# Four of 128 stores of a decode-attention backward kernel sent as 126 + 2 partitions, to choose the DMA engines that carry them

## The chip, the cores and the metric

The kernel runs on one core of one Trainium2 chip. The metric is the device time of that core in microseconds (us), as the median of several executions. "Engine" is used for two things: the compute engines (PE is TensorE, DVE is VectorE, ACT is ScalarE, POOL is GpSimd, SP is SyncE) and the 16 DMA engines that move data for the core. Where it matters I write "DMA engine".

## The reference, cut to what matters

```python
B, H, Sq, Sk, D = 2, 32, 1, 8192, 128          # q, grad_out: 1 row a head; k, v: 8192 rows a head; bf16
def forward(q, k, v):
    scores = einsum("bhqd,bhkd->bhqk", q, k) * D ** -0.5
    return einsum("bhqk,bhkd->bhqd", softmax(scores), v)
out, vjp = jax.vjp(forward, q, k, v)
return (out, *vjp(grad_out))                    # out, dq, dk, dv
```

There are 64 heads. For each the kernel loads 2 MB of k and 2 MB of v and stores 2 MB of dk and 2 MB of dv: 268 MB in and 268 MB out.

## The kernel before

Each tile holds one head's k or v: 128 partitions of 64 x 128 bf16, 16 KB a partition. I call such a partition a row. The outer product that gives dk or dv overwrites the same tile, which is then stored. There are 12 tile slots, so the load for head i + 6 waits until the store of head i has landed. SyncE issues the loads and GpSimd issues the stores.

```python
NTILE = 12
load_eng = nc.sync
store_eng = nc.gpsimd
...
def load(i, w, pieces=(NCH,)):
    t = kvp.tile([P, NT, D], BF16, tag=f"kv{slot_of(i, w)}", name="kvt")
    h.tile[w] = t
    src = (v_v if w else k_v)[i]
    ...
        pin(load_eng.dma_start(out=t[:, n0:n1, :], in_=src[:, n0:n1, :]))
...
def outer(i, w, c, ends):
    pin(nc.vector.tensor_tensor(out=h.tile[w][...], in0=h.qb[w][...], in1=h.pair[w][...], op=ALU.mult))
    if c + 1 in ends:
        ...
        dst = (dv_v if w else dk_v)[i]
        pin(store_eng.dma_start(out=dst[:, b0:b1, :], in_=h.tile[w][:, b0:b1, :]))
...
        if (i := at(O1 + NCH)) is not None and i + AHEAD < BH:
            load(i + AHEAD, 0)
        if (i := at(O0 + NCH)) is not None and i + AHEAD < BH:
            load(i + AHEAD, 1)
        if x := within(O1):
            outer(x[0], 1, x[1], last if x[0] == BH - 1 else whole)
        if x := within(O0):
            outer(x[0], 0, x[1], last if x[0] == BH - 1 else whole)
```

## Time and profile before

| | before |
|---|---|
| time, median (range) | 1304.45 us (1304.21 to 1306.08, 4 runs) |
| span of the profiled run | 1303.1 us |
| busiest compute engine (PE) | 89% |
| the two data queues, share of 16 DMA engines | 48.9% + 48.7% |
| mean DMA rate | 414 GB/s |

These are lines of the page of the kernel before: the busy time of each compute engine, the DMA's busy tenths and rate in 40 equal slices of the span, the queues (packets, MB, share), and two groups of DMA issues (last column: median us from issue to landing).

```profile
span 1303.1 us, 42566 instructions
PE 1154.0 (89%) x19268; PEld 873.0 (67%) x19268; DVE 937.5 (72%) x2122; ACT 974.8 (75%) x641; POOL 72.4 (6%) x142
...
DMA  9999999999999999999999999999999999999965
GB/s 390 423 427 427 427 427 427 428 426 430 427 427 427 427 427 429 427 428 427 429 427 427 429 427 424 418 420 425 421 416 420 419 421 421 418 421 422 394 281 206
...
q1 hardware_dynamic: 19040, 268.51, 48.9%
q0 software_dynamic: 19296, 268.44, 48.7%
...
out_dram<-kvt POOLq DMA_DIRECT2D x126, 2048.0 KB, 40.4
kvt<-in_v_dram SPq DMA_DIRECT2D x64, 2048.0 KB, 49.3
```

The DMA is busy from the second slice to the last two. For 24 slices it moves about 427 GB/s (423 to 430 in slices 2 to 24), then about 420, and the last three slices show 394, 281 and 206. So the DMA bounds the kernel. The busy digits 6 and 5 of the last two slices are means over 16 engines: some have run out of work before others, as the landings of the last store below show (3 us on fifteen engines, 10 on one).

Waits on the kernel before: the queue of SyncE (columns: engine and line, what it waited for, us in total, times, longest).

```profile
SPq L89 <- DMA out_dram<-kvt: 1140.6, 116, 24.2
```

```profile
POOL out_dram L390 <- DVE kvt L376: 1186.8, 127, 32.2
```

SyncE spends nearly the whole span waiting for stores to land, since a landed store is what frees a tile for the next load; it never waits longer than 24.2 us.

The trace has one semaphore update for each DMA engine and DMA, 16 in all. Their times after the issue show the engines apart (my reading of the trace, us, in order of landing):

```
before, load  issued at 1003.10: 12 12 12 12 12 13 14 | 28 28 29 29 29 30 31 32 | 49
before, store issued at 1001.50: 12 12 13 13 13 14 16 | 19 20 20 21 21 21 21 21 | 42
before, last store at   1291.64: 3 (fifteen engines)                            | 10
```

Seven engines are early, eight are later, and one is alone at the end. I call it the slow engine. It is the one that is still busy when the kernel ends.

Its packets can be followed in the trace, because on a DMA engine that has work the next packet's record mostly starts 3 or 4 ns before the end of the one before. Which packet follows which is sometimes ambiguous, so what is said below of single engines is a reading, not a view of the profile. The slow engine's packets have no gap from about 140 us to the end. A 16 KB row takes 0.607 us from start to start at full pace.

### The profile page before, as it was taken

To read this page: it belongs to the slowest core of one execution; us is meant where nothing else is said; L and a number is where in the kernel's file an instruction comes from. 1 tells how busy PE (TensorE), PEld (TensorE's weight loads), DVE (VectorE), ACT (ScalarE), POOL (GpSimd) and SP (SyncE) were. 2 spreads that over 40 slices of the span, in tenths; PEclk is the share of its full clock that TensorE was granted. 3 is DMA by queue.
4 is the path that set the end of the run, shared out by engine and by line. 5 is a ranking of instruction groups with operands and counts; after the bars stand their busy time and mean duration, and the time that the engine had idled before them with its cause. 6 is when DMAs were issued, how large, how long until landed. Compare 5 with 4: busy or idle time off the path is not lost.

```text
span 1303.1 us, 42566 instructions
## 1 busy us (share of the span) xinstructions
PE 1154.0 (89%) x19268; PEld 873.0 (67%) x19268; DVE 937.5 (72%) x2122; ACT 974.8 (75%) x641; POOL 72.4 (6%) x142
## 2 busy tenths in 40 slices
PE   6999998889898888988989888989898898888984
PEld 5777776667676666666766666667676676666662
DVE  2888887677776777767777677676776767777776
ACT  6888887777787777777778777777777777777771
POOL 0000000000000000000000000000000000000001
PEclk9999999899898999989989999898898989999986
DMA  9999999999999999999999999999999999999965
GB/s 390 423 427 427 427 427 427 428 426 430 427 427 427 427 427 429 427 428 427 429 427 427 429 427 424 418 420 425 421 416 420 419 421 421 418 421 422 394 281 206
DMA packets 38517, 539.67 MB, mean 414 GB/s; under 512 B 4544, under 2 KB 4544, under 8 KB 5824
## 3 DMA queue, kind: packets, MB, share of 16 engines
q1 hardware_dynamic: 19040, 268.51, 48.9%
q0 software_dynamic: 19296, 268.44, 48.7%
q8 instruction: 150, 2.46, 0.7%
q14 instruction: 31, 0.25, 0.0%
HBM read 268.47 MB, written 268.47 MB: 412 GB/s over the span
## 4 chain that ended last, share of the span: by engine, by line
issue 80%; DMA 11%; POOL 4%; DVE 2%; PE 1%; POOLq 0%; SPq 0%; DVEq 0%
DMA kvt<-in_v_dram 8%; POOL out_dram L390 4%; DMA out_dram<-kvt 3%; DVE kvt L376 1%; PE tp L166 1%; POOLq L390 0%; PE acc L321 0%; DVE sel L344 0%; PE dpw L177 0%; SPq L89 0%; SPq L96 0%; DVE sel L338 0%; PE sw L177 0%; PE acc L358 0%; DVE pair L252 0%
## 5 line engine op out<-in xcount | busy, mean ns | idle before, releaser
L168 ACT COPY ev<-tp 128x2048 bf16<-128x2048 bf16 x512 | 954.0, 1865 | 300.3 <-PE tp L166 290.6
L166 PE MATMUL tp<-ident_bf,kvt 128*128 128x128 bf16 x8192 | 573.4, 226 | 108.9 <-DMA kvt<-in_v_dram 91.1
L376 DVE TENSOR_TENSOR kvt<-qb,pair 128x2048 bf16<-128x2048 bf16 x512 | 621.1, 1214 | 0.2
L166 PEld LDWEIGHTS <-kvt 128*128 128x128 bf16 x8192 | 501.4, 102 | 116.2 <-DMA kvt<-in_v_dram 95.8
L177 PEld LDWEIGHTS <-ev 128*128 128x128 bf16 x8192 | 242.8, 96 | 211.2 <-issue 164.4
L321 PE MATMUL acc<-kvt,dS_pad 128*64 128x512 bf16 x1024 | 177.2, 430 | 1.3 <-DVE dqT L361 1.3
L321 PE MATMUL acc<-kvt,E_pad 128*64 128x512 bf16 x1024 | 159.8, 392 | 0.0
L177 PE MATMUL dpw<-qdT,ev 128*128 128x1 bf16 x4096 | 140.9, 164 | 12.0 <-DVE qb L159 10.7
L189 DVE TENSOR_REDUCE mp<-sw 128x1 f32<-128x64 f32 x64 | 14.3, 224 | 186.5 <-PE sw L177 186.5
L344 DVE SCALAR_TENSOR_TENSOR sel<-acc,diag,sel 128x128 f32<-128x128 f32 x384 | 134.6, 351 | 13.6
L177 PE MATMUL sw<-qdT,ev 128*128 128x1 bf16 x4096 | 142.5, 164 | 1.1 <-ACT ev L168 1.1
L390 POOL DMA_DIRECT2D out_dram<-kvt x134 | 71.3, 532 | 1219.2 <-DVE kvt L376 1186.8
L321 PEld LDWEIGHTS <-dS_pad 128*64 128x64 bf16 x1024 | 38.5, 113 | 26.9 <-issue 9.4
L229 DVE CAST E_pad<-E_f 128x64 bf16<-128x64 f32 x64 | 12.5, 195 | 60.6 <-ACT E_f L220 60.6
L321 PEld LDWEIGHTS <-E_pad 128*64 128x64 bf16 x1024 | 36.3, 108 | 21.0 <-issue 0.2
L358 PE MATMUL acc<-ones,sel 128*128 128x1 f32 x256 | 43.3, 239 | 6.2 <-DVE sel L344 6.2
L264 PE MATMUL dpw<-ld,ones 128*128 128x1 f32 x256 | 46.3, 250 | 0.1
L338 DVE TENSOR_SCALAR sel<-acc,diag 128x128 f32<-128x128 f32 x128 | 44.0, 344 | 0.0
L358 PEld LDWEIGHTS acc<-ones,sel 128*128 128x128 f32 x256 | 39.0, 193 | 7.3 <-DVE sel L344 7.3
L235 DVE CUSTOM_DVE_ANT_0 junk<-E_f,dpw 128x64 bf16<-128x64 f32 x64 | 14.1, 220 | 40.2 <-PE dpw L177 40.2
L159 DVE CAST qb<-dpw 128x128 bf16<-128x128 f32 x128 | 35.4, 277 | 6.0 <-PE dpw L150 6.0
L264 PEld LDWEIGHTS dpw<-ld,ones 128*128 128x128 f32 x256 | 38.2, 188 | 0.5 <-DVE ld L235 0.5
(42 smaller groups left out, 303.2 us busy)
## 6 DMA issues: line engine op xcount, KB each, us to landing
out_dram<-kvt POOLq DMA_DIRECT2D x126, 2048.0 KB, 40.4
kvt<-in_v_dram SPq DMA_DIRECT2D x64, 2048.0 KB, 49.3
kvt<-in_k_dram SPq DMA_DIRECT2D x63, 2048.0 KB, 49.4
out_dram<-kvt POOLq DMA_DIRECT2D x8, 512.0 KB, 11.3
kvt<-in_k_dram SPq DMA_DIRECT2D x2, 512.0 KB, 4.5
kvt<-in_k_dram SPq DMA_DIRECT2D x1, 1024.0 KB, 7.1
out_dram<-nat SPq DMA_DIRECT2D x2, 16.0 KB, 5.0
qd_nat<-in_q_dram SPq DMA_DIRECT2D x1, 16.0 KB, 6.8
```

Source lines behind the costliest of these rows:

```text
L159: pin(nc.vector.tensor_copy(out=h.qb[w][:], in_=h.qbp))
L166: pin(nc.tensor.transpose(tp[:, t, :], src[:, c * CH + t, :], ident_bf[:]))
L168: pin(nc.scalar.copy(out=ev[:], in_=tp[:]))
L177: nc.tensor.matmul(dst[:, c * CH + t : c * CH + t + 1], lhsT=ev[:, t, :], rhs=qdT[:, w, i : i + 1], start=True, stop=True,)
L189: pin(nc.vector.reduce_max(out=h.mp[:], in_=h.s, axis=AX.X))
L264: nc.tensor.matmul(out, lhsT=ones[:].to_broadcast([P, P]), rhs=col, start=True, stop=True)
L321: nc.tensor.matmul(h.acc[w][g : g + CW, :], lhsT=wts[:, n0 : n0 + CW], rhs=rows[:, n0 : n0 + QT, :].rearrange("p n d -> p (n d)"), start=( ...
L338: nc.vector.tensor_scalar(out=h.sel[:], in0=block, scalar1=diag[:, 0:1], scalar2=None, op0=ALU.mult)
L344: nc.vector.scalar_tensor_tensor(out=h.sel[:], in0=block, scalar=diag[:, b : b + 1], in1=h.sel[:], op0=ALU.mult, op1=ALU.add,)
L358: nc.tensor.matmul(h.acc[w][:, 0:1], lhsT=h.sel[:], rhs=ones[:], start=True, stop=True)
L376: nc.vector.tensor_tensor(out=h.tile[w][:, n0 : n0 + CH, :].rearrange("p n (e t) -> p n e t", t=2), in0=h.qb[w][:] .rearrange("p (e t) -> ...
L390: pin(store_eng.dma_start(out=dst[:, b0:b1, :], in_=h.tile[w][:, b0:b1, :]))
```

## The change

```diff
+            if w == 0 and i % 14 == 9 and ends is whole:
+                spread(dst, h.tile[w])
+            else:
+                pin(store_eng.dma_start(out=dst[:, b0:b1, :], in_=h.tile[w][:, b0:b1, :]))
+
+    def spread(dst, t):
+
+        def eighths(ap, m):
+            parts = ap[P - 1 : P].rearrange("p (e m n) d -> p m e (n d)", e=8, m=2)
+            return parts[:, m]
+
+        pin(store_eng.inc_swdge_sem([], [], mode="reset_dge_cursor"))
+        pin(store_eng.dma_start(out=eighths(dst, 0), in_=eighths(t, 0)))
+        pin(
+            store_eng.dma_start(
+                out=dst[: P - 2], in_=t[: P - 2], max_dma_last_dim=NT * D
+            )
+        )
+        pin(load_eng.dma_start(out=eighths(dst, 1), in_=eighths(t, 1)))
+        pin(load_eng.dma_start(out=dst[P - 2 : P - 1], in_=t[P - 2 : P - 1]))
```

## The prediction

Engines 6 and 7 were to be left out. The "it" that "keeps about 29 us" is the slow engine. The sum is 1304.2 - 19.4 + about 1 = 1286 us; its 19.4 us, an estimate from the pitch in the trace (4 stores x 8 rows x 0.607 us), counts only if the slow engine is left out.

> **What bounds the kernel.** The DMA engines. The page's slices show DMA at 9 of 10 up to the last two; the two data queues take 48.9% and 48.7% of 16 engines' span. PE is 89% busy, others less. SyncE's queue waits 1140.6 us for stores to land, as tiles are reused.

> Not all 16 engines bind. The trace has 16 semaphore updates for each DMA, one an engine. For loads and stores issued around 100 us they lie within about 4 to 8 us; around 1000 us seven land 12 to 14 us after a load's issue, eight after 28 to 32, and one alone after 49. The gap grows until about 800 us; then the slow engine holds back tile reuse, and GB/s falls from 427 to 420. Every 8 loads take 77.8 us before (128 packets of 16 KB at a pitch of 0.607 us) and about 81 after. I conclude that one engine is busy from 4 us to the end with about 48 us more than the fastest, and 20 us more than the next eight. It alone sets the time.

> **What the change does.** An ordinary store gives an engine 8 rows, 8 x 0.607 = 4.86 us. [...] So engines 6 and 7 save 4 x 4.86 = 19.4 us and the others gain 4 x 0.607 = 2.4 us, plus little for the two rows. No trace names an engine; [...] Then it keeps about 29 us over the fastest and the next eight about 24: it still binds, and all of the 19.4 us counts.

> **What it costs.** SyncE sends the rest in order: after a load that waits for the store of dv of the same head, and the next load waits for these rows to land. They lie behind the loads queued on the slow engine (49 us): four times the next load comes some 40 us late, and the load queue runs empty for about 2 us. The fast engines idle then, at no cost, as they were ahead; the slow one has four stores queued. I allow 0 to 2 us for each of the four.

> **Prediction.** 1304.2 - 19.4 + about 1 = 1286 us, 1.4% faster; range 1279 to 1304. Chances: faster by over 2% 0.05, within 2% 0.92, slower 0.03.

> **What would show it.** Right: in the stores concerned 14 engines take 9 rows and two take one small piece; after each of the four places the spread of landings falls to a few us, and one load is issued about 40 us late; the mean rate rises to about 420 GB/s. Wrong: the last landing still trails by about 20 us on the same schedule.

> **What would make it wrong.** The slow engine is not 6 or 7, or the store of 126 partitions goes over 16 engines after all: then 1304 to 1310. The late loads starve PE or drain the store queue as well, up to 10 us each. Or the next eight engines bind sooner.

## More of the kernel before

GpSimd waits for DVE's outer products, never for a DMA.

On the slow engine the store packets take a median of 0.644 us while it also reads loads, where the median of the other engines is 0.611.

## The result and the profile after

| | before | after |
|---|---|---|
| time, median (range) | 1304.45 us (1304.21 to 1306.08, 4 runs) | 1308.98 us (1308.24 to 1309.07, 4 runs) |
| ratio after / before, 95% interval | | 1.0031 (1.0013 to 1.0048) |
| span of the profiled run | 1303.1 us | 1306.5 us |
| granted PE clock in it | 0.944 | 0.955 |

An interval that leaves out 1 shows a difference. Ratios here and below are the mean time of one kernel's runs over that of the other's in the same rounds, so they are not quite the ratio of the medians. The kernel is 0.3% slower, where 1.4% faster was predicted.

These are the lines of the page of the kernel after that answer to those of before, with the new groups of DMA issues (126 rows are 2016 KB; half of a row is 8 KB).

```profile
span 1306.5 us, 42590 instructions
...
DMA  9999999999999999999999999899999999999965
GB/s 389 423 426 427 428 427 427 427 427 428 427 426 428 429 425 428 420 414 427 426 429 428 427 425 424 364 427 427 428 428 428 427 423 421 370 429 428 428 275 206
...
q0 software_dynamic: 20064, 268.35, 48.6%
...
out_dram<-kvt POOLq DMA_DIRECT2D x122, 2048.0 KB, 47.8
out_dram<-kvt POOLq DMA_DIRECT2D x4, 2016.0 KB, 51.4
out_dram<-kvt POOLq DMA_DIRECT2D x4, 8.0 KB, 35.9
```

The last two slices are as before (275 and 206 against 281 and 206): the end still trails. The dips to 414, 364 and 370 are new. They follow three of the four places.

The next fence has the queue of SyncE in the kernel after, as waits; the two behind it show this queue's issues around the third place as a timeline (start in us, duration, line, transfer), first before, then after.

```profile
SPq L89 <- DMA out_dram<-kvt: 1140.3, 108, 43.8
```

```profile
809.98 0.33 SPq L89 DMA_DIRECT2D kvt<-in_v_dram  x1
820.22 0.33 SPq L89 DMA_DIRECT2D kvt<-in_k_dram  x1
830.44 0.33 SPq L89 DMA_DIRECT2D kvt<-in_v_dram  x1
840.54 0.33 SPq L89 DMA_DIRECT2D kvt<-in_k_dram  x1
```

```profile
805.50 0.33 SPq L89 DMA_DIRECT2D kvt<-in_k_dram  x1
805.93 1.56 SPq L409 DMA_DIRECT2D out_dram<-kvt  x1
807.54 0.42 SPq L410 DMA_DIRECT2D out_dram<-kvt  x1
843.57 0.34 SPq L89 DMA_DIRECT2D kvt<-in_v_dram  x1
844.02 0.36 SPq L89 DMA_DIRECT2D kvt<-in_k_dram  x1
844.55 0.33 SPq L89 DMA_DIRECT2D kvt<-in_v_dram  x1
848.85 0.33 SPq L89 DMA_DIRECT2D kvt<-in_k_dram  x1
```

Before, a load is issued every 10 us. After, the two stores that SyncE sends (L409, L410) stop the loads for 36 us, and then three come within 1 us. That is the delay the prediction spoke of, and at first sight it looks like the culprit. It isn't, as the slow engine shows.

The landings of the 126-row stores at the third and fourth places (my reading, us after the issue):

```
after, 126 rows, issued at  769.59:  8 16 18 18 18 18 19 | 21 24 24 26 26 26 27 27 | 53
after, 126 rows, issued at 1052.72:  8 14 15 15 16 16 19 | 20 20 20 20 21 21 22 22 | 56
```

One engine still lands alone, 26 to 34 us behind the fifteenth. In each of the four places the packets on the slow engine include 18 of 8 KB. That is 9 rows of the 126-row store, each in two packets; on GpSimd's queue only that store has such packets (1008 in the trace, 4 x 126 x 2). At the third place they alternate with its load packets from about 806 to 822 us. Loads are queued on the slow engine until 842.3 us, when a piece from SyncE goes out behind them; its next load packet starts at 847.7 us, and store packets fill the 5 us between. So the slow engine was not left out; it got one row more than in an ordinary store.

How many rows the slow engine has moved, loads and stores together, confirms both halves:

| rows done by the slow engine | before | after |
|---|---|---|
| by 1000 us | 1572.3 | 1572.0 |
| by 1200 us | 1888.8 | 1887.6 |
| at its end | 2048.25 at 1301.15 us | 2052.75 at 1304.29 us |

At equal times it has done the same within 1.2 rows, so the stalled loads cost it next to nothing. It ends 3.1 us later because it had 4.5 rows more: four ninth rows, and four times two pieces of 1 KB. At 0.63 us a row (midway between its loads' and its stores' pace) that is an estimated 2.8 us. The two profiled spans differ by 3.4 us, so this is nearly all of that loss; the medians differ by 4.5 us, and the rest was not traced. The loss is the change's own bookkeeping on the wrong engine.

Two DMA engines did get nothing of the 126-row stores. In their place the trace shows small filler packets of 4 bytes, 18 on each of the two, and one on each of the eight that took no eighth of the row. Those make 4 x (2 x 18 + 8) = 176, which is what the queue's packet count shows: 20064, against 19888 for data and semaphore packets alone. The pair with fillers was the same at each place, and none of the two had taken an eighth. So the 126 rows had not started eight engines further on than the eighths, as that would have left out two engines that took eighths. That they started where the eighths started is shown below, by experiments 5, 8 and 9.

So the first half of the expectation agrees with the trace: the 126 rows went to 14 engines, 9 rows each, and two engines had 18 fillers each. The second half, that a transfer in eight pieces moves the cursor by eight, does not.

### The profile page after: what moved, and what is told of

Read it like the earlier page. It is cut to its first block, busy times and chain, and to the rows that moved or that the text cites. A ratio compares the mean times of both kernels' runs of the same rounds, so it can differ in the third digit from the quotient of the medians.

```text
span 1306.5 us, 42590 instructions
## 1 busy us (share of the span) xinstructions
PE 1133.2 (87%) x19268; PEld 860.8 (66%) x19268; DVE 935.3 (72%) x2122; ACT 975.3 (75%) x641; POOL 76.2 (6%) x146
## 3 DMA queue, kind: packets, MB, share of 16 engines
q0 software_dynamic: 20064, 268.35, 48.6%
## 4 chain that ended last, share of the span: by engine, by line
DMA 40%; issue 28%; PE 17%; another core or an unknown queue 6%; DVE 5%; POOL 2%; ACT 1%; SPq 0%; POOLq 0%; ACTq 0%
DMA kvt<-in_v_dram 20%; DMA kvt<-in_k_dram 10%; DMA out_dram<-kvt 9%; PE tp L166 7%; PE acc L321 4%; DVE kvt L376 3%; PE sw L177 2%; PE dpw L177 2%; POOL out_dram L393 1%; DVE sel L344 1%; ACT ev L168 1%; PE dpw L264 1%; DMA qd_nat<-in_q_dram 1%; DVE sel L338 0%
## 5 line engine op out<-in xcount | busy, mean ns | idle before, releaser
L166 PE MATMUL tp<-ident_bf,kvt 128*128 128x128 bf16 x8192 | 560.0, 223 | 120.0 <-DMA kvt<-in_v_dram 96.7
L166 PEld LDWEIGHTS <-kvt 128*128 128x128 bf16 x8192 | 490.6, 101 | 127.3 <-DMA kvt<-in_v_dram 100.6
L321 PE MATMUL acc<-kvt,dS_pad 128*64 128x512 bf16 x1024 | 169.9, 414 | 0.8 <-DVE dqT L361 0.8
```

The costliest lines, as they stand in the source:

```text
L166: pin(nc.tensor.transpose(tp[:, t, :], src[:, c * CH + t, :], ident_bf[:]))
L321: nc.tensor.matmul(h.acc[w][g : g + CW, :], lhsT=wts[:, n0 : n0 + CW], rhs=rows[:, n0 : n0 + QT, :].rearrange("p n d -> p (n d)"), start=( ...
```

## The experiments

The letters in the expectations name the theories as they stood when each text was written; A is "the slow engine was not in the pair left out, and the rest costs next to nothing". The text before each says what was at issue. What an expectation says that the cursor does, or which engines a transfer leaves out, is the theory under test; the results follow it. The time before is that of the same rounds. All kernels gave correct outputs.

### 1. Which pair is left out, if nothing resets the cursor

Eight stores of 126 rows, without reset, the other two rows from GpSimd in 16 pieces each. If the cursor moves by 14 from one such store to the next, the eight stores leave out eight different pairs, and one of them has the slow engine.

```diff
-            if w == 0 and i % 14 == 9 and ends is whole:
+            if w == 0 and i % 7 == 2 and i > 2 and ends is whole:
...
-        pin(store_eng.inc_swdge_sem([], [], mode="reset_dge_cursor"))
-        pin(store_eng.dma_start(out=eighths(dst, 0), in_=eighths(t, 0)))
         pin(store_eng.dma_start(out=dst[: P - 2], in_=t[: P - 2], max_dma_last_dim=NT * D))
-        pin(load_eng.dma_start(out=eighths(dst, 1), in_=eighths(t, 1)))
-        pin(load_eng.dma_start(out=dst[P - 2 : P - 1], in_=t[P - 2 : P - 1]))
+        for p in (P - 2, P - 1):
+            pin(store_eng.dma_start(out=cut(dst, p, 16), in_=cut(t, p, 16)))
```

> Eight stores of dk (heads 9, 16, ... 58) go as 126 partitions from GpSimd, with no reset and no piece ahead; the two rows left go from GpSimd in 16 pieces each. What it is for: which turn of the cursor leaves out the slow engine. Theory A (the cursor moves by 14 with each such store, mod 16, and the slow engine simply was not one of the two left out before): the eight stores leave out eight different pairs, so in exactly one of the eight the slow engine gets 18 tiny packets in place of 18 packets of 8 KB, and its lag behind the others falls there by 5 to 8 us (its own 4.9 less and the others' 0.6 more), while in seven it grows by about 0.6. Time about 1304 + 7 x 0.6 - 5 = 1304, within 3. Rival B (14 engines are always the same ones, with no wrap): the lag never falls, and the time is about 1304 + 8 x 0.6 = 1309.

Measured: 1311.49 us (before 1304.71; ratio 1.0052, 1.0026 to 1.0078). The slow engine took 18 packets of 8 KB in seven of the eight stores and none in the sixth. If the cursor moves by 14 with each such store, it stands after five at 5 x 14 = 70, which is 6 modulo 16, and the sixth leaves out positions 4 and 5. Positions are counted from where the cursor starts or is reset to. So, if it does, the slow engine is one of 4 and 5.

### 2 and 3. Does the part that SyncE sends cost the time?

Experiment 2 lets GpSimd send all leftovers. Experiment 3 has only SyncE's part: every DMA engine gets its usual 8 rows, but 16 of the rows, one an engine, come from SyncE.

```diff
# experiment 2
-        pin(load_eng.dma_start(out=eighths(dst, 1), in_=eighths(t, 1)))
-        pin(load_eng.dma_start(out=dst[P - 2 : P - 1], in_=t[P - 2 : P - 1]))
+        pin(store_eng.dma_start(out=eighths(dst, 1), in_=eighths(t, 1)))
+        pin(store_eng.dma_start(out=cut(dst, P - 2, 16), in_=cut(t, P - 2, 16)))
# experiment 3: in place of the whole body of spread
+        for eng, r0, r1 in ((store_eng, 0, P - 16), (load_eng, P - 16, P)):
+            pin(eng.dma_start(out=dst[r0:r1], in_=t[r0:r1]))
```

> As the changed kernel, but all of the two leftover rows go from GpSimd (half a row in eighths, half a row in eighths again, one row in sixteenths), none from SyncE. Theory A (the slow engine is not left out and gets 9 rows for 8; what SyncE sends late costs nothing): still slower than before by 2 to 5 us, 1306 to 1309, and the gap of 38 us between loads at the four places is gone. Rival C (the late loads are what costs): back to 1304 or below it, 1285 to 1304.

> The part with SyncE alone: the same four stores go as 112 partitions from GpSimd (7 rows on each of 16 engines) and 16 from SyncE (1 row on each), so no engine has more or less to do, but the next load still waits behind them. Theory A: loads come 38 us late at four places, and the time is 1304 to 1306. Rival C: the whole loss of the change is seen here, 1308 to 1312.

Measured, experiment 2: 1310.66 us (1308.35 to 1311.51; before 1304.71; ratio 1.0043, 1.0024 to 1.0062). Taking SyncE out of it gained nothing, so SyncE's part is not why the change failed. The time was slightly above what A allowed. The swap is not clean: sent from GpSimd, the leftovers made GpSimd wait 108 us in all for landings (4.4 us in the kernel after). The rows done by the slow engine are the stronger evidence.

Measured, experiment 3: 1313.13 us (1309.95 to 1316.19; ratio 1.0057, 1.0027 to 1.0088), some 8 us more than before, where A expected next to nothing. This is a miss. Its four runs fall into two pairs, near 1310 and near 1316 us, which nothing here explains; the profile is of a run of 1315.94 us. These are its waits and its timeline on the queue of SyncE at one of the places, in the columns used above:

```profile
SPq L89 <- DMA out_dram<-kvt: 1116.4, 91, 72.8
```

```profile
1081.23 0.33 SPq L89 DMA_DIRECT2D kvt<-in_k_dram  x1
1081.65 0.44 SPq L398 DMA_DIRECT2D out_dram<-kvt  x1
1152.05 0.33 SPq L89 DMA_DIRECT2D kvt<-in_v_dram  x1
1152.48 1.00 SPq L89 DMA_DIRECT2D kvt<-in_k_dram  x1
1153.65 1.65 SPq L89 DMA_DIRECT2D kvt<-in_v_dram  x1
...
```

By my reading SyncE's store includes a row on the slow engine, which lies behind the loads queued there. The next load comes 70 us later, and eight loads then come within 10 us. Here the slow engine did lose work: at 1200 us it was about 13 rows behind the kernel before (my reading). So a stall of 36 us passed unnoticed and one of 70 us did not. Late loads were a real cost here, some 8 us; the kernel after was merely spared it.

### 4 to 6. The pair 4 and 5, by smaller pieces

If each piece moves the cursor by one, two pieces of one row and then four pieces of another after a reset move it by 2 + 4 = 6. Then 126 rows would leave out 4 and 5. SyncE sends the rest in experiment 4, GpSimd in 5, and experiment 6 is 5 with six such stores.

```diff
         pin(store_eng.inc_swdge_sem([], [], mode="reset_dge_cursor"))
-        pin(store_eng.dma_start(out=eighths(dst, 0), in_=eighths(t, 0)))
+        send(store_eng, P - 1, 2, 0)      # 2 pieces of one row
+        send(store_eng, P - 2, 4, 0)      # 4 pieces of one row
         (126 rows as in the change)
-        (the rest, by SyncE)
+        send(load_eng, P - 1, 2, 1)       # experiments 5 and 6: store_eng
+        send(load_eng, P - 2, 4, 1)
# experiment 6: six stores
-            if w == 0 and i % 14 == 9 and ends is whole:
+            if w == 0 and i % 9 == 4 and i > 8 and ends is whole:
```

> As the changed kernel (four stores, SyncE sends the rest), but two pieces and then four pieces ahead of the 126 partitions set the cursor to 6, so that engines 4 and 5 are left out in place of 6 and 7. Theory A (the mechanism of the prediction holds, only the engine was wrong: the sweep left the slow engine out at its sixth store, where the cursor stood at 70 mod 16 = 6): the slow engine has 32 rows less, its lag falls by about 5 us more than the others' at each of the four stores, and the time is 1284 to 1290, of which 0 to 3 us are lost to late loads. Rival C (the late loads cost as much as in the run with SyncE alone, 8 us): 1292 to 1296. Rival D (the engines next in order bind at once): 1300 or more.

> The same engines left out, with all of the two rows sent from GpSimd, so no load waits on SyncE. Theory A: 1283 to 1289; about equal to the run with SyncE where its late loads are free, faster by up to 8 us where they cost what they cost alone. Rival D: 1300 or more.

> Six such stores in place of four, from GpSimd alone. From the landings of before, the eight engines next in order trail the fastest by about 22 us at the end and gain 6 x 0.6 = 3.7, and the slow one would trail by 48 - 29 = 19. Theory A: the eight now bind, at about 1304 - 48 + 26 = 1282, that is within 3 us of the run with four stores and no longer 10 us better than it. If the slow engine alone mattered: 1275.

| | time (range), us | before | ratio (95%) | 8 KB packets on the slow engine, each place |
|---|---|---|---|---|
| 4 | 1310.53 (1310.2 to 1312.03) | 1304.24 | 1.0052 (1.0035 to 1.0069) | 18 |
| 5 | 1310.51 (1309.81 to 1311.51) | 1304.24 | 1.0049 (1.0034 to 1.0064) | 18 |
| 6 | 1314.33 (1313.38 to 1314.73) | 1304.24 | 1.0077 (1.0062 to 1.0092) | 18 |

All three missed. In the trace of 5, the two engines that took the two pieces are among the four that took the four pieces. The second transfer had started on the same engine as the first. So either the pieces don't move the cursor, or these sizes do not, or the reset does something else than I thought.

### 7 to 10. What keeps the cursor still: the number of pieces, or the reset?

Experiment 7 sends six pieces of one row ahead of the 126 rows, in case only powers of two leave the cursor where it is (theory E). Experiment 8 sends twelve and twelve. Experiments 9 and 10 have no reset, in case the reset is at fault (theory F): six pieces ahead and 6 + 3 + 3 behind in 9, and 4 + 4 ahead and 5 + 5 behind in 10. GpSimd sends everything.

```diff
# 7
-        pin(store_eng.dma_start(out=eighths(dst, 0), in_=eighths(t, 0)))
+        send(store_eng, P - 1, 0, 48, 6, 0)
# 8
+        send(store_eng, P - 1, 0, 48, 12, 0)
+        send(store_eng, P - 1, 0, 48, 12, 1)
# 9
-        pin(store_eng.inc_swdge_sem([], [], mode="reset_dge_cursor"))
+        send(store_eng, P - 1, 0, 24, 6, 0)
         (126 rows)
+        send(store_eng, P - 1, 0, 24, 6, 1)
+        send(store_eng, P - 1, 24, 36, 3, 0)
+        send(store_eng, P - 1, 24, 36, 3, 1)
# 10
-        pin(store_eng.inc_swdge_sem([], [], mode="reset_dge_cursor"))
+        send(store_eng, P - 1, 0, 16, 4, 0)
+        send(store_eng, P - 1, 0, 16, 4, 1)
         (126 rows)
+        send(store_eng, P - 1, 16, 36, 5, 0)
+        send(store_eng, P - 1, 16, 36, 5, 1)
```

> What is known: the slow engine is among the eight that take the eighths of the changed kernel, the two left out there are not among the eight, the four pieces of the runs that meant to leave out 4 and 5 go to engines that include those of the two pieces, and the slow one is not among them. Theory E: pieces for 2, 4 or 8 engines always start at the first engine and do not move the cursor, so 126 partitions after a reset always left out 14 and 15; the slow engine is one of 4 to 7. Here the reset is followed by a transfer in six pieces, which is no power of two: the 126 partitions then start at 6 and leave out 4 and 5. All from GpSimd. If the slow one is 4 or 5: at each of the four stores it takes no packet of 8 KB, and the time is 1283 to 1290. If it is 6 or 7, or if six pieces do not move the cursor either: 18 such packets on it each time, 1307 to 1312.

> The counterpart: two transfers of twelve pieces after the reset, so that the cursor stands at 24 mod 16 = 8 and the 126 partitions leave out 6 and 7, as the change meant. Theory E: exactly one of this run and the run with six pieces leaves out the slow engine and takes 1283 to 1290; the other takes 1307 to 1312. If neither does, small pieces never move the cursor. If the one that leaves it out is not faster than 1300, the mechanism of the prediction is wrong, not only the engine.

> What is known: in every run with the reset, all transfers of one burst (2, 4, 6, 8, 12 or 14 engines) began at the same engine, and the two left out by the 126 partitions were the same ones, never the slow one; in the sweep, which has no reset, the pair left out moved from store to store and held the slow engine at the sixth. Theory F: it is the reset that fails; after it the cursor no longer moves (or is put back), so every transfer begins at engine 0 and 14 and 15 are left out; without any reset the cursor moves by the number of engines used. Here: no reset; six pieces, the 126 partitions, six, three and three pieces, which adds up to 32, so each of the four stores starts at 6 and leaves out 4 and 5. Theory F: the slow engine (4 or 5 by the sweep) takes no packet of 8 KB at any of the four, and the time is 1283 to 1292. Theory G (small pieces never move the cursor, only wide transfers do): starts are 0, 14, 12 and 10, the slow engine takes 18 packets each time, 1307 to 1312.

> The control: the same without a reset, but four and four pieces ahead (and five and five after), so that 6 and 7 are left out, as the change meant. Theory F: another pair than in all runs with the reset is left out, the slow engine is not in it, 18 packets of 8 KB on it each time, 1307 to 1312. If the slow engine is 6 or 7 instead, this run takes 1283 to 1292 and the run with six pieces does not.

| | time (range), us | before | ratio (95%) | 8 KB packets on the slow engine, each place |
|---|---|---|---|---|
| 7 | 1310.86 (1309.07 to 1311.93) | 1304.52 | 1.0049 (1.0031 to 1.0066) | 18 |
| 8 | 1309.75 (1309.39 to 1311.51) | 1304.52 | 1.0046 (1.0027 to 1.0066) | 18 |
| 9 | 1312.04 (1311.77 to 1312.32) | 1305.0 | 1.0053 (1.0037 to 1.007) | 18 |
| 10 | 1311.85 (1311.72 to 1312.5) | 1305.0 | 1.0053 (1.0038 to 1.0068) | 18 |

By E exactly one of 7 and 8 would have left out the slow engine, and neither did, so E falls. In 8 both transfers of twelve pieces went to the same twelve engines. In 9, after the first 126 rows, three of the engines that took the six pieces took those of both threes as well. In 9 and 10, without the reset, the pair did move from one 126-row store to the next, but the pieces between them did not move it; so F falls. What is left, for experiments 1 to 10: pieces of one row, 2 to 12 of them, started at the cursor and left it there (18 packets of 8 KB on the slow engine at every place of 4 to 10), and the 126-row stores of 1, 9 and 10 moved it (in 1, 18 such packets in seven stores and none in the sixth). The next theory (I) was that the cursor moves only where partitions are shared out, and not where a single partition is cut.

### 11 to 13. Moving the cursor with transfers of several partitions

In experiment 11 the two leftover rows are sent ahead of the 126 as three transfers of two partitions, each a third of their columns. If each moves the cursor by 2, the 126 rows leave out 4 and 5. Experiment 12 reaches the same 6 by another way: five transfers of 14 partitions and one 256-byte column. Experiment 13 is the rival that tests the pair itself: four transfers of two partitions make 8, and the 126 rows leave out 6 and 7. That is what the change had meant to do.

```diff
# 11: in place of the eighths and of SyncE's part
         pin(store_eng.inc_swdge_sem([], [], mode="reset_dge_cursor"))
+        send(P - 2, P, 0, 22)             # partitions 126, 127; column blocks 0 to 21
+        send(P - 2, P, 22, 43)
+        send(P - 2, P, 43, NT)
+        send(0, P - 2, 0, NT)             # 126 partitions
# 12
+        for n in range(5):
+            send(0, 14, n, n + 1)
+        send(0, P - 2, 5, NT)
+        send(14, P - 2, 0, 5)
+        row(P - 2)
+        row(P - 1)
# 13
+        for n in range(0, NT, 16):
+            send(P - 2, P, n, n + 16)
+        send(0, P - 2, 0, NT)
```

> What is known: no transfer cut from a single partition's row (2 to 12 pieces) has moved the start of the next transfer, with the reset or without; the 126-partition stores of the sweep have, from store to store. Here the two leftover rows go first as three transfers of two partitions each (columns in thirds), then the 126 partitions; reset as in the changed kernel. Theory I (the cursor moves where the partitions themselves are shared out, not where one row is cut): start 6, engines 4 and 5 left out, slow one among them, no packet of 8 KB on it at the four stores, 1283 to 1290. Theory J (powers of two never move it) or K (nothing moves it inside a burst): start 0, 18 packets each time, 1306 to 1312.

> Five transfers of 14 partitions and one column block of 256 bytes each, then the 126 partitions without those five columns; reset as in the changed kernel. Each of the six is of the kind that moved the cursor in the sweep (14 engines), so the last should start at 5 x 14 = 70 mod 16 = 6 and leave out 4 and 5. Theories I and J: the slow engine takes no packet of the big store at any of the four places, 1284 to 1292 (some 30 small packets more on each engine). Theory K (inside a burst nothing moves): 18 packets each time, 1307 to 1314.

> As the fast run with three transfers of the two leftover rows, but four of them (columns in quarters), so that the cursor moves by 8 and the 126 partitions leave out 6 and 7: the change as it was meant, without SyncE. If the engine was wrong as well as the cursor: the slow engine takes 18 packets of 8 KB at each of the four stores, 1306 to 1312. If only the cursor failed (the slow one is 6 or 7, and three transfers moved it by other than 6): 1285 to 1291.

| | time (range), us | before | ratio (95%) |
|---|---|---|---|
| 11 | 1288.67 (1288.47 to 1288.96) | 1304.27 | 0.9884 (0.9868 to 0.9901) |
| 12 | 1293.41 (1292.73 to 1295.57) | 1304.27 | 0.9923 (0.9908 to 0.9938) |
| 13 | 1314.83 (1313.7 to 1316.66) | 1305.01 | 1.0073 (1.0058 to 1.0088) |

This is about the gain that was predicted, 15.6 us in experiment 11. Experiment 12 gained 10.9 us; it sends nine transfers a place where 11 sends four, and GpSimd waits 250 us in all for landings (156.4, 53.4 and 40.3 us at its three store lines). That these waits make the difference was not isolated. The slow engine had no 8 KB packet at any of the four places in 11; in 13 it had 18 at each. In 11 the pair left out is the one that took the third small transfer, as a count of positions with steps of 2 says: at the first place its two packets of 5376 bytes, at 230.2 and 235.3 us, are followed by 4-byte fillers alone. So the slow engine took a third of a row at each place and none of the 126. These are the landings of the 126-row store at the third place in 11 and in 13, then those of a later store, of a load and of the last store in each:

```
11, 126 rows, issued at  768.63: 12 13 14 14 14 15 18 35 43 43 44 44 44 46 47 47
13, 126 rows, issued at  788.20:  7  7 13 13 13 13 13 13 13 13 13 14 16 16 17 47
11, store,    issued at 1186.01: 22 24 25 26 27 28 31 49 53 54 55 55 55 56 58 58
13, store,    issued at 1192.68: 28 28 28 28 30 30 31 32 32 32 33 33 33 34 37 69
11, load,     issued at 1105.24: 18 18 18 18 18 18 18 18 18 19 19 19 19 20 20 20
13, load,     issued at 1181.53: 14 15 15 15 16 16 16 16 16 16 16 16 16 17 17 19
11, last store,          1274.72: 3 (eight engines)  5 5 5 5 6 7 9 9
13, last store,          1302.83: 3 (fifteen engines)              9
```

In the stores of 11 no engine lands alone any more. In 13 one still does, 30 us after the fifteenth at the third place, and at the end of the kernel. The loads do not tell the two apart: in 13 too a load lands on all 16 engines within 5 us, and in 5 and 8, which also kept the slow engine at work and were slower than the kernel before, the median load lands after 20 to 21 us. With small transfers from GpSimd the backlog stands in the stores and not in the loads (median landings below: stores 59.4 and 61.3 us, loads 20.8 and 19.0; before 40.4 and 49.3); why was not looked into. The lines of the page of experiment 11, and two of 13:

```profile
span 1286.4 us, 42598 instructions
...
GB/s 387 424 427 428 426 426 427 427 427 426 428 427 429 428 427 425 424 426 425 427 426 427 425 422 408 420 428 426 428 428 428 427 415 422 425 428 427 428 410 241
...
out_dram<-kvt POOLq DMA_DIRECT2D x122, 2048.0 KB, 59.4
kvt<-in_v_dram SPq DMA_DIRECT2D x64, 2048.0 KB, 20.8
```

```profile
out_dram<-kvt POOLq DMA_DIRECT2D x122, 2048.0 KB, 61.3
kvt<-in_v_dram SPq DMA_DIRECT2D x64, 2048.0 KB, 19.0
```

The mean rate is 420 GB/s in 11, against 414 in the kernel before and 410 in 13. The packet count of GpSimd's queue agrees too: 20320 is 312 more than its 20008 data and semaphore packets, and a 126-row store with 36 fillers plus three two-partition transfers with 14 each (of 8 bytes, 168 in all) make 78 at each of four places, 312 in all.

Experiment 13 shows that the change would have failed even with a cursor at 8, as 6 and 7 was the wrong pair. It also cost more than its extra rows explain: 9.8 us, where four ninth rows at 0.63 us are an estimated 2.5. Its waits on GpSimd show something that the kernel before has not (the other runs that send all leftovers from GpSimd have it too, the fast 11 with 167 us among them):

```profile
POOL out_dram L393 <- DMA out_dram<-kvt: 44.1, 7, 10.9
POOL out_dram L400 <- DMA out_dram<-kvt: 37.6, 4, 9.6
```

GpSimd now waits for earlier stores to land before it can issue the next one. The stores use eight semaphores in turn (read from the trace), and each small transfer takes one of the eight as a 2 MB store does. That this is the reason for the waits is inferred from the order in which semaphores come round; no run isolated it. The rate of 13 dips to 351 and 314 GB/s in two slices near the places.

### 14 and 15. A version that beats both, and one step further

Experiment 14 is 11 with the right half of the two rows sent by SyncE, so that the small transfers are half as large and SyncE's part is tried again with the right pair. Experiment 15 is 11 with six such stores. If the slow engine still set the end, two more such stores would have gained again.

```diff
# 14
+        send(P - 2, P, 0, 11)
+        send(P - 2, P, 11, 22)
+        send(P - 2, P, 22, 32)
+        send(0, P - 2, 0, NT)
+        pin(load_eng.dma_start(out=dst[P - 2 :, 32:], in_=t[P - 2 :, 32:]))
# 15: experiment 11 with
-            if w == 0 and i % 14 == 9 and ends is whole:
+            if w == 0 and i % 9 == 4 and i > 8 and ends is whole:
```

> The fast run with the right half of the two leftover rows sent by SyncE in place of GpSimd; the rest as there (cursor at 6, slow engine left out). If late loads cost nothing, as the prediction said: within 2 us of the fast run, 1287 to 1291. If they cost what SyncE alone cost beside whole stores: 1294 to 1299.

> The fast run with six such stores in place of four. With four, at the end the slow engine lands within 1 to 5 us of the eight next in order and about 13 us after the fastest seven. If the eight bind now: 1287 to 1291, no gain, and the slow engine is no longer last. If the slow engine alone still bound: 1279.

| | time (range), us | before | ratio (95%) |
|---|---|---|---|
| 14 | 1288.19 (1287.08 to 1288.44) | 1305.01 | 0.9865 (0.9849 to 0.9882) |
| 15 | 1301.07 (1298.37 to 1302.32) | 1305.01 | 0.9963 (0.9947 to 0.998) |

Experiment 14 has the lowest time found, 16.8 us under the kernel before; its interval overlaps that of 11, so the two are not told apart. Its queue of SyncE at the third place, and its longest wait:

```profile
808.59 0.33 SPq L89 DMA_DIRECT2D kvt<-in_k_dram  x1
809.01 0.88 SPq L416 DMA_DIRECT2D out_dram<-kvt  x1
825.39 0.35 SPq L89 DMA_DIRECT2D kvt<-in_v_dram  x1
```

```profile
SPq L89 <- DMA out_dram<-kvt: 1135.2, 117, 24.5
```

The stall is 16 us here, against 36 in the kernel after and 70 in experiment 3. SyncE's rows have fewer loads ahead of them: a load issued at 1104.24 us lands on all 16 engines 17 to 19 us later. As 13 has such short load landings too, this need not come from the right pair.

Experiment 15 missed its expectation: it is slower than 11, where about the same or some 10 us less was expected. Near its end two engines trail the rest (the store issued at 1261.32 us lands on fourteen within 17 us and on these two after 23 and 28); whether the slow engine is one of them could not be read with certainty. These are the waits on GpSimd:

```profile
POOL out_dram L393 <- DMA out_dram<-kvt: 156.8, 22, 12.0
POOL out_dram L400 <- DMA out_dram<-kvt: 72.0, 9, 9.1
```

GpSimd waits for landings 31 times, 229 us in all. Experiment 11 had 167 us of such waits in 22 times and was not slower for it, so the sum alone doesn't give the 12 us between the two. Where those come from stays open.

## Why the prediction was wrong

1. "It alone sets the time." Right. Taking 32 rows from this one engine (and giving it about one row's worth of small pieces) gained 15.6 us (experiment 11) and 16.8 us (14); adding 4.5 rows to it made it end 3.1 us later (the change).
2. "So engines 6 and 7 save 4 x 4.86 = 19.4 us ... all of the 19.4 us counts." The size was nearly right for the engine that it should have been: 80 to 87% of it came. In 11 the store issued at 1186.01 us lands on seven engines after 22 to 31 us and on the other nine after 49 to 58, with none apart. So it seems that the slow engine had come level with the eight next in order before all of the saving was used; the pieces given back to it took a little as well. The predicted 1286 us is within 3 us of what the idea gives when it is carried out (1288 to 1289).
3. "So engines 6 and 7 save" took for granted that the reset and the eighths put the cursor at 8. **This is the step that failed.** The number of engines was right, 14 with 9 rows each (18 packets of 8 KB on the slow one at each place). But the eighths of a single row did not move the cursor; the 126 rows began where the eighths had begun, at position 0, and so, counted on from there, left out 14 and 15. In experiments 5, 8 and 9 transfers cut from one row started on the same engine as the one before (in 8 both transfers of twelve pieces went to the same twelve engines). In experiments 1, 11 and 12 transfers which share out 126, 2 or 14 partitions did move it; a step of that many positions modulo 16 fits where the slow engine was left out in all three (1: no 8 KB packet on it in the sixth store; 11: none at any place, 15.6 us gained; 12: 10.9 us gained), and where it was not in 13 (18 packets at each place). Whether the number of engines or that of partitions modulo 16 counts cannot be told from these.
4. The same words took for granted that the slow engine is one of 6 and 7. This failed too, independently: with the cursor moved to 8 in earnest (13: four steps of 2) the slow engine kept its 9 rows, 18 packets of 8 KB at each place, and the time was 1314.83 us. It is one of positions 4 and 5 (1, 11 and 12 agree); which of the two was not tried. No trace here names an engine, so which engine number position 0 has is not known.
5. "The others gain 4 x 0.607 = 2.4 us." Right in size, and as the slow engine was one of these others, this and the small pieces (together 4.5 rows, 3.1 us at its end) are nearly all of the 3.4 us between the profiled spans.
6. "Four times the next load comes some 40 us late ... I allow 0 to 2 us for each." Right for this change: 36 us at the third place, and the slow engine did the same rows in the same time within 1.2. Its load queue was empty for about 5 us there, not 2, but stores filled it, as the prediction said they would. It does not hold for longer stalls: those of 70 us cost about 8 us in all (experiment 3).
7. Under "what would make it wrong" the prediction named "the slow engine is not 6 or 7 ... then 1304 to 1310", and 1308.98 lies in it. The range, which ended at 1304, left that case out. It rested on two facts that no trace showed, the cursor's step and the engine's number, and either one false was enough.
8. Not foreseen: with small transfers of its own GpSimd waits for landings (82 us in experiment 13, 167 us in 11, 229 us in 15, 250 us in 12, none before). What these waits cost was not isolated.

## What to carry to other kernels

Here one DMA engine of 16 ended alone, and taking 32 rows of 16 KB from it gave 16 of the 19 us computed from its pace. In such a case, first find out by a sweep which engine it is and check in the trace that the transfer really left it out, by the packet sizes that only this transfer has, before trusting any arithmetic on a cursor. Transfers that waited behind the loads on the slow engine stalled the queue that issues loads: stalls of 36 us cost nothing here, those of 70 us about 8 us in all. And more of the same need not bring more: six such stores took 1301.07 us, four 1288.67.
